# A DeltaNet and MLP-mixer kernel: 130 of the first 900 steps stand elsewhere in the order of issue

## The chip, the core and the metric

The kernel runs on one core of a Trainium2 chip. The metric is the device time of one execution in microseconds (us): 623.53 before, the median of three runs (623.19 to 623.9).

## What is computed

The reference is a DeltaNet recurrence on q, k, v (batch 4, heads 8, sequence 768, head width 48) with a gate beta, followed by an MLP mixer on its output, laid out as (4, 768, 384).

```python
for t in range(S):                      # k normalised to length 1
    y[:, :, t] = einsum('bhd,bhde->bhe', q[:, :, t], state)
    v_old = einsum('bhde,bhd->bhe', state, k[:, :, t])
    state += beta[t] * outer(k[:, :, t], v[:, :, t] - v_old)
x = y as (B, S, H*D)
u = x + (relu(x^T @ w_tok1) @ w_tok2)^T        # token part
out = u + relu(u @ w_ch1) @ w_ch2              # channel part
```

## The kernel before

**Tiling.** The recurrence is walked in chunks of 64 positions. A *unit* is two chunks (128 positions) of one batch for all heads, so there are 24 units, six per batch. For each unit the kernel makes products of keys and queries with themselves, inverts a triangular matrix per chunk and head, and then carries the state from one chunk to the next with small products (64x48 and the like). The mixer of a batch follows when its units are written; its channel part is a Strassen-like sum of fewer large products.

**What sets the order.** Every piece of work is a Python generator, a *job*, that issues a few instructions and then yields; each stretch between two yields is a *step*. A table of words at the end of the kernel function (`order = """..."""`, from L1779) says whose next step is issued: `i0*2` means two steps of job i0. The instructions of all steps go, in this order, into the queues of their engines, and every engine runs its queue in order: PE (products), DVE, ACT and POOL (elementwise work), SP (which issues the DMAs). A waiting instruction holds up all behind it on its engine. Steps are counted from 0 here: r8.5 is the sixth step of job r8.

**The jobs that matter here.**

- k*u*, v*u* load keys, queries and values by DMA (L420, L444); b loads beta (L252) and turns it with products and an ACT copy (L261).
- p*u* normalises the keys of a unit: squares on ACT (L539), sums on DVE (L542), roots on ACT (L547, L548), the factors cs on DVE (L551, L552), the scaled mask mb (L574, on DVE for the first units and on POOL later), the scaled keys (L592), and the turned keys and queries through PE (L562, L582) and ACT (L566, L587).
- c*x*, d*x*: the products of the two chunks of a unit (four steps of L511 on PE), and their masking out of PSUM on DVE (L517), in the fifth step.
- t*u* brings the masked products to the layout of the inversion (ACT L674, DVE L677, POOL L679; from t7 on by DMA through DRAM, L686), i*n* is the inversion, a chain on DVE of a product (L747) and a sum (L751) per step after a transpose (L731), f*u* brings the result back (ACT L697, DVE L703, POOL L706), h*u* and j*u* join the inverted blocks (PE L781, L794, L855, L896; ACT L785, L799, L822, L873).
- r*x* is the recurrence of a chunk: p_k (L924) on PE, rw_t on DVE (L931), products (L944, L948) on PE, a copy on ACT (L954), a second group of products (L962, L963) on PE, the state ss_t on DVE (L971), the output on ACT (L976). In a chunk with ten steps the first group is step 5 and the second step 7.
- w*n* loads a weight piece: DMA (L280), two ACT operations (L286, L287), a DVE shift (L289), a POOL addition (L293); pieces from w18 on have sums of pairs on DVE (L318) behind these.
- m0 is the mixer of batch 0, whose first four steps are the products L1597 (four each in the trace).
- x, z (L235, `keep_warm`) and Y (L245, `warm_tiles`) are products of zeros, whose result is never read.

The tables, buffers and functions are the same before and after; POOL also clears two tiles once, one for the turned blocks (L652) and z16 (L619), in the course of the first t and h steps. Tiles named "prep" in PSUM come from a pool of two buffers.

Of the kernel before, what the change touches and what calls it, by code (L numbers as in the profile page):

```python
# [23 lines left out]
def kernel(  # L24
# [41 lines left out]
    B, H, S, D = q.shape  # L66
# [117 lines left out]
    t11 = const.tile([128, NB, HB], FP32, name="t11")  # L184
# [17 lines left out]
    w1 = const.tile([128, NCH, DTOK], FP32, name="w1")  # L202
    w2 = const.tile([128, NDH, S], FP32, name="w2")
# [407 lines left out]
    t16 = spare[:, cuts[1] : cuts[2]].rearrange("s (q t b) -> s q t b", q=2, t=QB)  # L611
# [1175 lines left out]
    w6 p5 p3 p5 j0*3 f1*2 h1*5 j0*2 w8*2 w17 f2 h2*3 v0 t4*2 w17 r0*5 p6 h2*2 c5*2  # L1787
    v1 w11*2 j1 p5 k7*2 c5 k7 c5 r0 c5 r0*2 w14*2 v1 w11*2 k7*2 p7 d5*5 r1*5 w14*2
    p6*2 t5 j1 t5*2 r1*2 j1 j2 p7 h3*2 r1*3 p6*3 i1*2 r2*5 k8*2 f3*2 w9 k9*3 j1*2
    v2*2 i1*3 j2*2 r2*2 f3 i1*2 p6*3 w16 v2 w16*3 r2*2 h3 r2 i1 d6 r3*5 i1*2 w9*3  # L1790
    v2 d6 h3 v2 w0 h3*2 r3 h3 d6*2 w0 d6 j3 c6*5 r3*4 w0 j2 w0 p8*2 j2 r4 p8 r4*4
    k9*3 j3*2 r4*2 i1*2 w24 i1*2 p7*7 r4 c7 r4 r5*5 k10 p9 k10 p9 c7 r4 c7*3 i1
    w5*2 p7 r5*2 w24*3 r5*3 j3*2 i1 r6*4 w26 v3*5 p9 k11 r6 d7*5 w26*3 p8*3 t6*2
    r6*2 w5*2 p8*4 v4*2 t6 i1 r6*3 h5*2 h4*2 k10*2 f4*3 c8*2 k10 p10 w28*2 c8*2 r7
    c8 r7*3 d8*4 p9 d8 w28 h4*5 p9 t6 r7*2 j4 w28 p9*3 r7*2 p9 w7 d9 w7 v4*2 f5*2
    w27*2 w7*2 d9*4 c9*2 f5 c9*3 t7*2 t8 r7*2 t7*2 j4*2 v4 p10*2 h5 r8*3 w29 t8*3
    w29 w27*2 r8*2 w29*2 q3 w29 j4*2 r8 w22*4 t9*3 r8*3 p9 r9 p10 r9*3 t9 v5 h5*3
    j5 i2 r9 w4*2 r8 h5 i2*5 w4 i2 w19*2 k10 w32 p10*2 w32 v7 k12 m0*2 k11 k12 q0
    v5*3 p10*2 r9*2 j5*2 k11*3 i2*2 r9 w4 i2 j5 i2*3 p10 v5 r9*2 d10*3 r10 v7*2 j5
    i2*2 r10*4 w12 i2 k12 i2*2 m0 w32 k11 k12 w32 r10*2 m0 p11 k12*4 w19 p11 r10  # L1800
    c10 r10 c10 r10 w33 d10*2 q2 Y r11*4 v7 r11*3 w19 c10 q1 w30 c10 r11 k12*2
    i2*3 r11 v6*4 i2*5 m0*3 i2*5 q5 i2 m0 p11*4 c10 p11 m0 p11*2 m0*2 k12*2 w12
    m0*3 v6 f6*3 w12 d11 c11*2 d11*2 c11 w33 c11 d11*2 j6 p12 w12 m0 w33 w30*3
    p12*2 f7*3 j6*2 m0 c11 j7 f6 f8 w27*2 f8 j7 f8 w15 f7 m0 w29 w33 w29 j7 r12*4
    w31 j8 p11 t10*3 r12 Y r12 f9 j8 f9 w21 p12 r12 f8 r13*2 w15*2 r12 w15 r13*3
# [81 lines left out]
```

## Time and profile before

| | before |
|---|---|
| median of the runs | 623.53 us |
| the profiled execution | 626.48 us, span 624.7 |
| granted TensorE clock, mean | 0.973 |
| PE busy | 594.3 us (95%) |
| DVE busy | 466.1 us (75%) |
| ACT busy | 256.6 us (41%) |
| POOL busy | 110.2 us (18%) |

Times in the profile count from the span's start. A row of a timeline gives the start, the length, the engine, the line and the operation with what it writes and reads, and in brackets how long its engine had stood idle before it and what ended that. A row of the chain of waits gives the start and the length of a piece of the chain that ended last. A row of the stretches gives the stretch, the busy time of each engine, the granted clock (1.00 is full), the share of the DMA engines that was busy, and GB/s. In the first 125 us PE is not always busy, and its clock is cut in six windows of 3.4 us and multiples of it, from 29.6 us on.

### The profile page before, as it was taken

The page shows a single profiled execution, that of the slowest core. Times are in us where ns is not written, and L with a number is a line of the kernel's source. Part 1 is how long each engine was busy: PE and PEld are TensorE (multiplying, and loading weights), DVE is VectorE, ACT ScalarE, POOL GpSimd, SP SyncE. Part 2 cuts the span into 40 slices and gives each one's busy share as a digit, 9 for nine tenths or more (in the row PEclk, how much of TensorE's full clock was granted, in tenths as well). Part 3 has the DMA queues.
Part 4 walks back from the last instruction along what each step waited for, and adds up shares of the span by engine and source line. Part 5 has one row for each costly group of instructions (what it writes and reads, how often), then busy time and mean ns, then how long its engine had stood idle before and what let it go on. Part 6 is the DMA issues. An engine that isn't in the chain of part 4 may idle for free.

```text
span 624.7 us, 20909 instructions
## 1 busy us (share of the span) xinstructions
PE 594.3 (95%) x8733; PEld 519.7 (83%) x8733; DVE 466.1 (75%) x1160; ACT 256.6 (41%) x682; POOL 110.2 (18%) x150
## 2 busy tenths in 40 slices
PE   8489898899999999999999999999999999999998
PEld 5467776667898988977888888896699999999997
DVE  4986876986889845697567986866688898675874
ACT  7748787448522344213551305423252241404200
POOL 2346355215311121003020130011000000000000
PEclk9978897999999999999999999998999999999999
DMA  9566567657653244554544443134102012020001
GB/s 220 125 140 146 143 151 192 137 139 177 129 113 71 64 103 91 102 116 96 104 74 123 93 88 76 35 80 120 32 2 39 1 17 48 14 52 13 14 26 50
DMA packets 154605, 55.52 MB, mean 89 GB/s; under 512 B 129648, under 2 KB 148976, under 8 KB 154512
## 3 DMA queue, kind: packets, MB, share of 16 engines
q1 hardware_dynamic: 154512, 54.20, 38.3%
q8 instruction: 68, 1.11, 0.8%
q14 instruction: 25, 0.20, 0.1%
HBM read 41.19 MB, written 11.21 MB: 84 GB/s over the span
## 4 chain that ended last, share of the span: by engine, by line
PE 74%; DVE 10%; DMA 4%; ACT 3%; issue 2%; SPq 2%; POOL 0%; ACTq 0%; DVEq 0%
PE p_c L1672 13%; PE p_r L1502 13%; PE p_o L1693 10%; PE p_a L1574 6%; PE p_b L1574 6%; PE p_g L511 3%; PE p_h L1612 3%; DVE x L751 2%; PE p L1597 2%; DVE sub L747 2%; PE p_k L924 1%; DMA x<-n_dram 1%; PE p_h L1242 1%; PE p_s L962 1%; PE p_y L1038 1%
## 5 line engine op out<-in xcount | busy, mean ns | idle before, releaser
L1672 PE MATMUL p_c<-u_t,wc 128*128 128x256 f32 x432 | 101.6, 386 | 0.6 <-issue 0.6
L1672 PEld LDWEIGHTS p_c<-u_t,wc 128*128 128x128 f32 x432 | 79.6, 190 | 11.9 <-issue 1.1
L1693 PE MATMUL p_o<-wc,r 128*128 128x192 f32 x360 | 64.6, 331 | 0.7 <-DVE xb L1632 0.7
L751 DVE TENSOR_TENSOR x<-x,sub 128x84 f32<-128x84 f32 (+24 forms) x178 | 59.6, 335 | 6.1
L747 DVE TENSOR_TENSOR sub<-x 128x84 f32<-128x84 f32 (+24 forms) x178 | 57.7, 324 | 8.1 <-DMA x<-n_dram 3.5
L1693 PEld LDWEIGHTS p_o<-wc,r 128*128 128x128 f32 x360 | 58.4, 190 | 2.3 <-DVE xb L1632 1.3
L1681 ACT ACTIVATE r<-p_c 128x512 f32<-128x512 f32 x36 | 21.5, 596 | 49.3 <-PE p_c L1672 43.9
L511 PE MATMUL p_g<-kq 48*64 48x128 f32 (+1 forms) x704 | 35.2, 288 | 3.0 <-ACT kq L587 3.0
L517 DVE TENSOR_TENSOR gm<-p_g,mb 128x512 f32<-128x512 f32 x44 | 28.9, 684 | 9.5 <-PE p_g L511 8.4
L484 POOL TENSOR_TENSOR v_st<-v_st,nrm 128x384 f32<-128x384 f32 x12 | 11.2, 931 | 132.4 <-DMA v_st<-in_v_dram 104.8
L511 PEld LDWEIGHTS p_g<-kq 48*64 48x64 f32 (+1 forms) x704 | 27.1, 141 | 7.9 <-ACT kq L587 4.0
L574 POOL TENSOR_TENSOR mb<-mask_c,cs 128x512 f32<-128x512 f32 x20 | 21.2, 1061 | 65.3 <-DVE cs L552 35.7
L293 POOL TENSOR_TENSOR wc<-w_f,d 128x384 uint32<-128x384 uint32 x24 | 24.6, 1030 | 43.3 <-DVE w_f L289 20.2
L1502 PE MATMUL p_r<-t_d,wc 128*128 128x192 f32 x160 | 28.8, 326 | 0.0
L1515 DVE TENSOR_TENSOR kq<-kq,p_r 128x384 f32<-128x384 f32 x40 | 21.1, 552 | 10.2 <-PE p_r L1502 8.3
L1515 DVE TENSOR_TENSOR gm<-gm,p_r 128x384 f32<-128x384 f32 x40 | 21.2, 552 | 8.1 <-PE p_r L1502 5.8
L400 DVE STREAM_TRANSPOSE kq<-pads 128x512 f32<-128x512 f32 x24 | 25.6, 1109 | 1.6 <-DMA pads<-in_k_dram 1.2
L1502 PEld LDWEIGHTS p_r<-t_d,wc 128*128 128x128 f32 x160 | 26.5, 190 | 0.0
L1693 PE MATMUL p_o<-wc,s 128*128 128x192 f32 x144 | 25.7, 330 | 0.7 <-DVE xb L1632 0.7
L1502 PE MATMUL p_r<-pads,wc 128*128 128x192 f32 x128 | 25.4, 326 | 0.0
L1693 PEld LDWEIGHTS p_o<-wc,s 128*128 128x128 f32 x144 | 23.3, 190 | 1.3 <-DVE xb L1632 1.0
L1632 DVE TENSOR_TENSOR xb<-xb,p_o 128x192 f32<-128x192 f32 x42 | 14.7, 349 | 12.7 <-PE p_o L1693 12.3
(315 smaller groups left out, 1390.6 us busy)
## 6 DMA issues: line engine op xcount, KB each, us to landing
d<-in_moe_w_ch_dram SPq DMA_DIRECT2D x24, 384.0 KB, 3.9
v_st<-in_v_dram SPq DMA_DIRECT2D x96, 48.0 KB, 2.7
out_dram<-xb SPq DMA_DIRECT2D x23, 192.0 KB, 2.1
kst<-in_k_dram SPq DMA_DIRECT2D x64, 48.0 KB, 2.6
n_dram<-gm SPq DMA_DIRECT2D x72, 32.0 KB, 2.4
pads<-in_k_dram SPq DMA_DIRECT2D x24, 96.0 KB, 3.0
pads<-in_q_dram SPq DMA_DIRECT2D x24, 96.0 KB, 2.7
gm<-w_dram SPq DMA_DIRECT2D x72, 32.0 KB, 2.1
```

Source lines behind the costliest of these rows:

```text
L293: nc.gpsimd.tensor_tensor(out=dst.bitcast(U32), in0=f, in1=lo, op=ALU.add)
L400: nc.vector.transpose(kq_of[p // 2][:, i, :, p % 2].rearrange("f p (s g) -> f p g s", g=G), rows_of[i].rearrange("s p (g d) -> s p g d", g ...
L511: nc.tensor.matmul(p_g[PAR[i ^ cc ^ swap(u)], p], kqt[f, p, cc, 0], kqt[f, p, cc])
L517: nc.vector.tensor_tensor(out=blocks(gm_of(u))[:, :, cc, D:GW].rearrange("s p (two n) -> s p two n", two=2), in0=p_g, in1=made[u][:, :, cc ...
L747: nc.vector.tensor_tensor(out=tmp, in0=by[0].to_broadcast(list(to.shape)), in1=by[1].to_broadcast(list(to.shape)), op=ALU.mult,)
L751: nc.vector.tensor_tensor(out=to, in0=to, in1=tmp, op=ALU.add)
L1502: nc.tensor.matmul(p[:, i], pieces[q // width][:, at : at + 128], f[f"u{n}"], start=first and i == 0, stop=True, skip_group_check=True,)
L1515: nc.vector.tensor_tensor(out=o, in0=o, in1=p, op=op_of(sign))
L1574: nc.tensor.matmul(p, a[:, i], w[:, i // 2, i % 2], start=first and i == 0, stop=True, skip_group_check=True,)
L1672: nc.tensor.matmul(p_c[:, k], piece_of(wc1, cb, f * 128)[:, f * 128 : (f + 1) * 128], u_t[:, cb], start=(cb == 0), stop=(cb == NCB - 1),)
L1681: nc.scalar.activation(r2[:, m], p_c, ACTF.Relu)
L1693: nc.tensor.matmul(p, a[:, m], wc2[:, m, j], start=(start and i == 0), stop=(i == NM - 1), skip_group_check=True,)
```

## The change

The order table is written anew. It has the same 2610 steps, and each job's steps keep their order; 130 steps, all among the first 900, stand elsewhere, and behind step 869 the table is the same word for word. Of the table the diff shows three pieces.

```diff
     order = """
-    w10 x*4 z w10*2 z w1*4 k1*3 z k1*3 z b p1 z p1 k0*6 p0*2 b*2 p1 w2 p0*5 p1*2
+    w1*4 w10 x z w10*2 z k1*3 z x k1*3 z p1 z p1 k0 b k0*5 p0*2 b p1 b w2 p0*5
...
-    p4*2 t2*3 x t3*2 p4*2 x t3 i0*2 w13 p4*2 w18 w17*2 i0 k4 i0*9 p4 i0*2 p4*2 c4
-    k8 c4*3 w13*2 w6*2 k5*2 v0 k6 k5*2 i0*2 d4*2 k5 x z d4*3 c4 z*2 p5*2 k5 t4 p5
-    h0 h1 h0 w8*2 h1 Y i0 f0 Y p4 f1 h2*2 p5*3 f0*2 w6 h0*5 k6*5 p6 z f2*2 k8*3 p5
+    w18*2 i0*2 w13 p4*2 i0 k4 z*4 i0*8 w13 i0 w13 p4 w6 i0 w6 i0 p4*2 c4 k8 c4*3
+    k5*2 v0 k6 k5*2 i0*2 d4*2 k5 x d4 w8 d4 w8 d4 c4 p5*2 k5 t4 h0 h1 h0 p5 h1 i0
+    f0 p4 f1 p5 h2 p5 h2 p5 f2 f0*2 w6 f2 h0*5 k6*5 p6 k8*2 p5*2 k8 p5 w6 p3 j0*2
...
-    w29 w27*2 r8*2 w29*2 q3 w29 j4*2 r8 w22*4 t9*3 r8*3 p9 r9 p10 r9*3 t9 v5 h5*3
-    j5 i2 r9 w4*2 r8 h5 i2*5 w4 i2 w19*2 k10 w32 p10*2 w32 v7 k12 m0*2 k11 k12 q0
+    q3 w27*3 j4*2 r8 w29 t9*3 r8 t9 r8*2 w22 w29 m0*2 r8 w29 r8 p9 w29 r9*4 v5
+    h5*2 p10*2 h5 j5 r9 w22*3 i2 h5 i2 r8 i2 j5 i2 w4 i2 j5 i2 w4 i2 w4 k10 w19
...
```

At the first inversion POOL ran, before:

```order
L293 TENSOR_TENSOR wc_119<-w_f,d_282 128x384
L574 TENSOR_TENSOR mb<-mask_c,cs 128x512
L293 TENSOR_TENSOR wc_119<-w_f,d_403 128x384
L652 MEMSET r_124 128x32x16
L619 MEMSET z_571 128x2304
L592 TENSOR_TENSOR gm<-kst_98,cs 128x8x48
```

and now:

```order
L293 TENSOR_TENSOR wc_119<-w_f,d_276 128x384
L293 TENSOR_TENSOR wc_119<-w_f,d_403 128x384
L574 TENSOR_TENSOR mb<-mask_c,cs 128x512
L652 MEMSET r_124 128x32x16
L619 MEMSET z_583 128x2304
L592 TENSOR_TENSOR gm<-kst_98,cs 128x8x48
```

The first L293 is w18's, the one on d_403 w13's. w13's addition now stands ahead of p4's mask mb; and on DVE the shift that w13's addition waits for (L289 on d_403) moves from behind the inversion's step on 52 elements to behind its second step on 100 elements (L751 with shape 128x2x5x10).

On PE, around the joins of the first three units (h0 and h1 are the L781 on wc_120, h2 the one on gm), there stood before:

```order
L562 MATMUL p_t<-ident,pads 128x128 x4
L582 MATMUL p_t<-ident,pads 128x128 x4
L511 MATMUL p_g<-kq 64x128 x12
L235 MATMUL p_warm<-warm 128x128
L235 MATMUL p_warm<-warm 128x512
L511 MATMUL p_g<-kq 64x128 x4
L235 MATMUL p_warm<-warm 128x512 x2
L781 MATMUL p_z<-r_124,wc_120 64x32 x32
L245 MATMUL p_warm<-warm 64x128 x8
L781 MATMUL p_z<-r_124,gm 64x32 x16
```

and now:

```order
L245 MATMUL p_warm<-warm 64x128 x8
L235 MATMUL p_warm<-warm 128x128 x2
L562 MATMUL p_t<-ident,pads 128x128 x4
L235 MATMUL p_warm<-warm 128x512 x4
L582 MATMUL p_t<-ident,pads 128x128 x4
L511 MATMUL p_g<-kq 64x128 x12
L235 MATMUL p_warm<-warm 128x128
L511 MATMUL p_g<-kq 64x128 x4
L781 MATMUL p_z<-r_124,wc_120 64x32 x32
L781 MATMUL p_z<-r_124,gm 64x32 x16
```

The products of zeros that stood around and between the joins (z.6 to z.8 and Y, and behind them z.9) now stand ahead of or between p4's two transposes.

On PE, behind the first group of products of chunk r8, the difference has this piece:

```order
+L948 MATMUL p_w<-rw_t,gm 64x48
+L1597 MATMUL p_1877<-xb,w_117 128x384
+L1597 MATMUL p_1878<-xb,w_117 128x384
```

These are the first of m0's products, steps m0.0 and m0.1, which stood behind r9's p_k and p10's first transpose; steps m0.2 and m0.3, which stood between the products of r10, now stand ahead of r10.

More of the change, by code (lines that the diff above doesn't have):

```diff
@@ L1799 @@
[L1799 to L1805, printed above, removed]
@@ L1834 @@
-    f18 m1*3 c23*3 f20*2 f18 c23 f18*2 c23 f19*3 v18 r30 t22*4 c23 t23 r30*4 t23*3
+    w1*4 w10 x z w10*2 z k1*3 z x k1*3 z p1 z p1 k0 b k0*5 p0*2 b p1 b w2 p0*5
+    p1*2 w10 p0*2 x w3 w2 c0*3 p0 d0 c0 d0 p1 c0 d0*3 w2 k2*3 v1 p1*2 w18 k2*2 z
+    p1*2 c1*2 d1 k2 p2*2 c1 t0 d1 c1*2 d1*3 p2*3 t0 p2 w2 p2*2 Y p2*2 c2*2 d2
+    c2*3 d2 k3*6 p3 d2*2 p3 x d2 t1*3 p3*3 x p3*4 c3 k4*2 w3 k4 w3 k4*2 k7 w3 w13
+    d3*5 v1*2 v0*2 c3*3 v0 c3 Y*2 t0 p4*2 t2*3 x w18 t3*2 w17 p4 w17 p4 x t3
+    w18*2 i0*2 w13 p4*2 i0 k4 z*4 i0*8 w13 i0 w13 p4 w6 i0 w6 i0 p4*2 c4 k8 c4*3
@@ new lines @@
+    k9*3 j3*2 r4*2 p8*2 i1*2 w24 i1*2 p7*7 r4 c7 r4 r5*5 k10*2 p9*2 c7 r4 c7*3 i1
+    w5*2 p7 r5*2 w24*3 r5*3 j3*2 i1 r6*4 w26 v3*5 p9 k11 r6 d7*5 w26*3 p8*2 t6*2
+    r6*2 w5*2 p8*5 v4*2 t6 i1 r6*3 h5*2 h4 k10 h4 k10 f4*3 c8 k10 c8 p10 w28*2
+    c8*2 r7 c8 r7*3 d8*4 p9 d8 w28 h4*5 p9 t6 r7*2 j4 w28 p9*3 r7*2 p9 w7 d9 w7
+    v4*2 f5*3 w27 w7*2 d9*4 c9*5 t7*2 t8 r7*2 t7*2 j4*2 v4 p10 h5 r8*3 w29 t8*3
+    q3 w27*3 j4*2 r8 w29 t9*3 r8 t9 r8*2 w22 w29 m0*2 r8 w29 r8 p9 w29 r9*4 v5
+    h5*2 p10*2 h5 j5 r9 w22*3 i2 h5 i2 r8 i2 j5 i2 w4 i2 j5 i2 w4 i2 w4 k10 w19
@@ new lines @@
+    p10*2 j5 v7 k12 k11 k12 q0 v5*3 w32 p10 r9 p10 r9 k11 j5 k11*2 i2*2 r9 i2*3
+    m0*2 i2 w32 v5 w4 p10 w19 r9*2 r10 v7*2 i2*2 r10*3 d10*3 c10 r10*2 w12 i2 k12
+    i2*2 k11 k12 r10 p11 k12*4 r10*2 c10 w32 r10 w32 w33 d10*2 q2 Y r11*4 v7
+    r11*3 w19*2 c10 q1 w30 c10 r11 k12 p11 k12 i2*3 r11 v6*4 i2*5 m0*3 i2*5 q5 i2
+    m0 p11*4 c10 p11 m0 p11*2 m0*2 k12*2 w12 m0*3 v6 f6*3 w12 d11 c11*2 d11*2 c11
+    w33 c11 d11*2 j6 p12 w12 m0 w33 w30*3 p12 f7*3 j6*2 p12 m0 c11 j7 f6 f8 w27*2
+    f8 j7 f8 w15 f7 m0 w33 j7 r12*3 w29*2 j8 p11 t10*2 f9 r12 w31 f9 t10 r12 Y
@@ new lines @@
+    r12 j8 w21 p12 r12 f8 r13*2 w15*2 r12 w15 r13*3 w31*3 Y r13*2 w33 j8 w21 m0
+    r13 q4 p12*4 r13*2 m0*2 r14 c12 f9 j9 r14*2 w21 t10 w20*2 v7 r14*2 c12*2 w33
+    c12 r14 v8 c12*2 r14*2 w25*2 j9 r14 r15 v8 w21 r14 r15 w25 r15*3 w25 k13*4
+    w20 k13*4 p13 k13*2 w20 v8*3 m0*2 p13 w25 p13 m0 r15 p13 r15 p13 w27 w25
+    k13*2 j9 m0*4 p13 f9 w23 t12*3 p13 t12 w25 r15*3 c13*6 w23 k14*7 r16*5 m0 p13
+    m0*3 w23*4 k14 r16*2 t11 t13*2 j9*2 t11*3 w33 p14 r16*2 p14*2 w31 m0*3 w31 m0
+    w31 m0 w23 r17*2 r16 t13 r17 t13 r17*2 p14*2 m0*2 p14 i3 k14*4 i3*3 k15 v9*2
@@ new lines @@
+    m0*3 v10 i3*5 k15 i3 r17 k15*2 p14 k15*3 m0 v10*2 i3 k15*2 m0*2 k15*2 i3*4
+    r17*4 k15 i3*2 p14 m0*2 i3*6 m0*4 r18 i3 r18*2 v9*3 r18*2 i3*8 m0*10 v10*2 m0
+    r18 c14*4 r18*2 m0*2 f10 c14 f10*2 f12*2 p15*3 m0*4 r18 r19 r18 r19*3 j10 f10
+    j10*2 f12 p15 f11*4 f12 r19 c14 r19 v11 p15*3 k16*7 j11 m0*2 r19*4 j11 j12
+    r20*3 k16*2 r20 m0 r20 k16*3 v11 m0 j11 r20*2 v11*2 p15 c15*2 p10 r20*2 c15
+    r20 c15*3 f13*3 p16 r21*5 m0 r21*2 p16*4 k17*7 p16 j12*2 p16 k17 r21*3 m0*3
+    r22 c16 r22*3 k17*4 v11 r22 c16*4 r22*2 m0 r22 t14 p17 f13 c16 t14 j13*2 t14
```

86 lines of the change are left out of this document (33 added, 53 removed).

## The prediction

> **What bounds the kernel now.** I read the page first: the granted clock in 40 slices of 15.6 us, in tenths, and the chain of waits by engine.
>
> ```profile
> PEclk9978897999999999999999999998999999999999
> PE 74%; DVE 10%; DMA 4%; ACT 3%; issue 2%; SPq 2%; POOL 0%; ACTq 0%; DVEq 0%
> ```
>
> PE carries three quarters of the chain, and DVE a tenth. The clock is cut only in the first seven slices (to about 109 us) and once near 435 us. So I cut the start into stretches (columns: stretch, busy us of PE, PEld, DVE, ACT, POOL, granted clock, DMA share, GB/s).
>
> ```profile
> 30.00:40.00 10.00, 7.67 (x44) 4.37 (x44) 8.35 (x30) 3.70 (x7) 2.99 (x3) 0.68 0.80 166
> 40.00:50.00 10.00, 8.47 (x159) 7.49 (x160) 7.64 (x13) 6.70 (x19) 4.99 (x6) 0.83 0.57 127
> 100.00:110.00 10.00, 7.98 (x93) 5.73 (x90) 5.37 (x21) 5.49 (x17) 4.38 (x5) 0.56 0.72 210
> 130.00:140.00 10.00, 10.00 (x72) 6.79 (x70) 7.47 (x24) 4.60 (x11) 3.05 (x4) 1.00 0.41 108
> ```
>
> From about 125 us on PE is hardly ever idle and at full clock, and the order of all steps from there is unchanged (the last moved step, p12's, lies at 141 us). What the change does is therefore a shift of the moment when that full stretch begins. Before it the kernel runs from one latency to the next, and each move is worth what it does to the chain at its place. I add these up in order of time; minus is earlier.
>
> **1. The start, up to the first inversion (i0).** A pair of weight pieces changes place, some products of zeros stand later, w3's last steps move from 13 to 23 us, and w18's ACT step moves from ahead of p4 to just ahead of t3.
>
> ```profile
> 16.72 0.55 DVE L542 TENSOR_REDUCE ksum<-ksq 128x8 f32<-128x384 f32 x1 [0.46 <-ACT ksq L539]
> 23.20 0.58 ACT L286 ACTIVATE d<-d 128x384 f32<-128x384 f32 x1
> 23.65 0.58 ACT L287 ACTIVATE d<-d 128x384 uint32<-128x384 uint32 x1
> 25.82 0.63 ACT L674 COPY r<-gm 128x256 f32<-128x256 f32 x1 [0.65 <-DVE gm L517]
> 26.51 0.85 POOL L679 COPY r<-gm 32x256 f32<-32x256 f32 x1 [0.66 <-ACT nrm L547]
> ```
>
> DVE works without a gap from 17 us to i0; its 0.46 us gap at 16.26, which ACT causes, closes when w3's two ACT operations leave that stretch, and p1's normalisation ahead of beta's copy brings perhaps 0.24. That would be -0.7. But i0 waits for POOL's copy L679, which waits for ACT's L674; ACT's 0.65 us of idle ahead of it now has to hold w18's pair, 1.03 us from 23.20 to 24.23. I take **-0.45**, between -0.7 and 0.
>
> **2. Inside i0, up to the first products of h0.** Here POOL and DVE get in each other's way.
>
> ```profile
> 27.39 1.25 DVE L731 STREAM_TRANSPOSE x<-r 128x1024 f32<-128x1024 f32 x1
> 28.67 0.84 DVE L747 TENSOR_TENSOR sub<-x 128x28 f32<-128x28 f32 x1
> 29.54 0.21 DVE L751 TENSOR_TENSOR x<-x,sub 128x28 f32<-128x28 f32 x1
> 39.40 1.37 DVE L759 TENSOR_SCALAR r<-r,even 128x512 f32<-128x512 f32 x1 [0.79 <-ACT r L758]
> 40.69 1.27 DVE L517 TENSOR_TENSOR gm<-p_g,mb 128x512 f32<-128x512 f32 x2
> 27.44 1.01 POOL L293 TENSOR_TENSOR wc<-w_f,d 128x384 uint32<-128x384 uint32 x1
> 28.41 1.04 POOL L574 TENSOR_TENSOR mb<-mask_c,cs 128x512 f32<-128x512 f32 x1
> 37.01 1.06 POOL L293 TENSOR_TENSOR wc<-w_f,d 128x384 uint32<-128x384 uint32 x1 [7.56 <-issue]
> 38.48 2.01 POOL L619 MEMSET z<- 128x2304 f32 x1
> 40.46 0.99 POOL L592 TENSOR_TENSOR gm<-kst,cs 128x384 f32<-128x384 f32 x1
> ```
>
> L747 at 28.67 ends at 29.51, as POOL's mb does (29.45): 0.84 instead of 0.21, so +0.63. L759 ends 0.28 after the memset z, about 0.9 late. The transpose L731 beside L293 and the PSUM-fed L517 beside L592 are not held. Now w13's POOL addition goes ahead of mb and both stand after i0's tenth step, where two-operand additions run one behind the other: each holds one of them, as mb held L747, so +0.8 twice (1.0 less some 0.25). The 0.63 at 28.67 goes. POOL's chain then starts some three us earlier than its 37.01, and z is done before L759, whose 0.9 goes: -0.63 + 0.8 + 0.8 - 0.9 = **+0.1**. This assumes that the memset, which falls on L747 and L751 now, does not hold them. No row shows that pair. If it holds one as it held L759, it and the L592 behind it cost up to 2.7 more. I take no hold: what the memset held is one operand at double rate (512 elements in the 0.28 us after its end, where L517 takes 0.64), not a sum of two.
>
> The Trainium skill, "SBUF — State Buffer", section "Who interferes with whom", says that a two-input DVE instruction contends with a GpSimd instruction that reads SBUF and not with one that only writes, while `tensor_scalar` can enter a two-port mode that is blocked by any. The mb, z, L731 and L517 rows agree with it; by it the term is +0.1, by L759's row taken alone up to +2.8.
>
> **3. From h0 to the first recurrence.** The two tiles of zeros (L245) leave their place between h1 and h2 on PE.
>
> ```profile
> 41.51 2.21 PE p_z L781 x64
> 43.71 1.75 PE p_warm L245 x16
> 45.46 1.53 PE p_z L781 x31
> ```
>
> In the chain of waits they are 1.75. Yet the zeros z that filled PE until shortly before h0 are gone as well (moved ahead of p4's second transpose, into idle time), so h0 and h1 will meet a half clock: 31 products took 1.53 there, 64 would take 3.1 instead of 2.21, +0.9. And ACT, which copies h0, h1, h2 and f0 to f2, has its own row of work from there to the first recurrence; I let it keep half of the remaining 0.85: **-0.4**, between -1.75 and +0.5.
>
> **4. r3 and r4.** d6's masking on DVE (step d6.4) moves behind r3.8. The "prep" PSUM buffer that it empties is the one j2's product writes next.
>
> ```profile
> 73.00 0.69 DVE L517 TENSOR_TENSOR gm<-p_g,mb 128x512 f32<-128x512 f32 x1 [0.76 <-PE p_g L511]
> 74.54 0.34 DVE L971 TENSOR_TENSOR ss_t<-ss_t,p_s 128x192 f32<-128x192 f32 x1
> 74.32 0.43 PE L896 MATMUL p_x<-gm,zst 32*32 32x32 f32 x15
> 75.69 0.25 ACT gm L822
> 78.82 0.60 ACT kq L587
> 79.46 0.43 PE p_g L511 x4
> ```
>
> L971 ends at 74.88, L517 then at 75.57: L896 starts 1.25 later, and ACT's L822, which waits behind its own 75.69, some 0.8 later. ACT works without a gap from there to 79.42, and r5 queues behind that. i1's eighth step goes into DVE's idle time ahead of r3 in return, worth up to 0.45. I take **+0.8**, between +0.3 and +1.3.
>
> **5. The place of i2.** m0's first eight products stand now between r8's two groups of products (steps r8.5 and r8.7) instead of behind r9; j4's last copy no longer waits for w29's pair on ACT; t9's writes go ahead of w22's load on SP.
>
> ```profile
> 99.65 0.55 ACT L286 ACTIVATE d<-d 128x384 f32<-128x384 f32 x1
> 100.09 0.54 ACT L287 ACTIVATE d<-d 128x384 uint32<-128x384 uint32 x1
> 100.65 0.75 ACT L822 COPY gm<-p_x 32x256 f32<-32x256 f32 x2
> 106.87 5.06 PE L1597 MATMUL p<-xb,w 128*128 128x384 f32 x8
> 117.57 1.49 PE p L1597 x4
> 103.37 0.34 PE L962 MATMUL p_s<-rw_t,gm 64*64 64x48 f32 x1 [0.41 <-ACT rw_t L954]
> 107.09 0.20 DVE sub L747
> 97.87:101.28 3.41, 2.63 (x94) 2.31 (x88) 2.67 (x6) 3.25 (x10) 2.55 (x5) 1.00 0.70 163
> 101.28:104.69 3.41, 2.42 (x62) 1.87 (x58) 0.79 (x3) 2.10 (x7) 2.41 (x3) 0.50 0.27 46
> ```
>
> L822 comes 0.75 earlier, r8.5's products end near 101.0 at full clock, then the eight take 2 x 1.49 = 3.0: r8's second group starts near 104.0 instead of 103.37, +0.65. Full clock saves some 0.8 on it and on r9's first products. DVE then does w29's two sums, p10's two, j5's transpose and r9.4 (about 1.9, an estimate at 0.3 to 0.4 for each of five, as such rows here have it), and w22's shift, before i2's first step: about 107.4 instead of 107.09, **+0.3**. The data of i2, earlier now, no longer matter. Whether the clock is full decides this term: the stretch of 3.41 us with PE busy 2.63 was followed by one at 0.50. It becomes busier by the 0.75 and by the first of the eight, so I take full clock. At half, the eight take 5.06, r8.5 and r8's second group 1.6 more, and i2 starts 3.3 later.
>
> **6. m0's next eight products, and the end of i2.** They move from between r10's steps, where the second row above (1.49, at 117.57) is one of two on the chain, to idle time ahead of r10. That is 3.0 off PE's chain, but DVE's inversion i2 runs without a gap beside it and r12 waits for its result as well; DVE's sum of work there is the same. I take **-0.4**, between 0 and -1.2.
>
> Everything else (w14 behind r1, beta's load behind k's on SP, the reorderings by one place) I put at nothing: at each the engine waits for another anyway, DVE for ACT at the start, ACT for PE behind r1; without that cover they are about 0.3 each, which the range holds.
>
> Sum: -0.45 + 0.1 - 0.4 + 0.8 + 0.3 - 0.4 = -0.05. The profiled execution took 626.48 (span 624.7 and 1.78 around it), 2.95 above the median of 623.53; I apply the sum to the median: **623.5**, no change. What a measurement of this kernel can tell from none is about 0.2%, 1.25 us.
>
> **The rivals.**
>
> *The half clock goes (faster).* Zeros and real products now stand in idle time at 26 to 31 us and at 101 to 104 us. Against my terms, PE may also keep its clock in one more of the half-clock windows: each costs up to 1.7 of PE's work, a pair late in the full stretch 3.4.
>
> ```profile
> 432.42:435.83 3.41, 3.16 (x64) 2.63 (x65) 3.34 (x10) 0.48 (x1) 0.00 (x0) 0.50 0.15 34
> ```
>
> The windows near 432 follow from a shift of the work against the window's beat. With h0 and h1 at full clock as well (-0.9) the sum is -0.05 - 0.9 - 1.7 = -2.65: 620.9. Against it: PE is still idle before h0.
>
> *The eight products at half clock (slower).* They stand ahead of r8's second group, and if the clock is cut at 101 us as before, i2 starts 3.3 later than before instead of 0.3 later, everything behind it too: -0.05 + 3.0, 626.5. It decides as soon as the stretch before stays near its 2.63 busy of 3.41. For it: the products ahead are tiny and ACT's wait remains; against it, the 0.75.
>
> *The memset holds i0 after all.* Then h0 comes up to 2.7 later, of which ACT's row of work hides a good half: +1.2, 624.7.
>
> **How the numbers follow.** No change as summed 0.40 (my terms carry about 1.5 either way: 0.13 faster, 0.20 same, 0.07 slower); clock kept 0.26 (0.24 faster, 0.02 same); eight products at half clock 0.21 (0.03 same, 0.18 slower); memset 0.13 (0.01, 0.07, 0.05). Together faster 0.38, same 0.32, slower 0.30. The range takes in the clock's gain and most of its loss: 620.3 to 626.4; the forecast's own is 622 to 625.
>
> **What would show it.** Right: in the new profile h0's products start within 0.8 us of 41.5 with no row of L245 behind h1; L747 steps of 1.0 beside w13 and mb but none of 2.0 beside the memset; r4 about 0.8 later against r3 than before; m0's first eight in 3.0 with clock 1.00 around 101 to 108 us; i2's first step within 1 us of 107. Wrong: clock 0.5 over the eight products, or a shift at 125 us that the rest does not keep.

## The result, and the profile after

The changed kernel takes 630.5 us (median of four runs, 628.69 to 633.21), the kernel before 623.36 in the runs beside it: 1.0118 times as long, with a 95% interval of 1.0081 to 1.0155. The forecast was no change, 623.5 us with a range up to 626.4. The kernel is slower, and lies outside the range. Medians, here and below, are of all executions, while the ratios leave out those more than 1.5% above their kernel's fastest, so the two need not agree to the tenth of a per cent.

The profiled execution took 631.57 us (span 629.6), 5.1 more than that of before. Its granted clock by slices of 15.7 us, and its chain of waits by engine:

```profile
PEclk9966799779999999999999999999999999999999
PE 68%; DVE 9%; DMA 3%; issue 2%; SPq 1%; ACT 1%; DVEq 0%; ACTq 0%
```

Against the row of before, slices 3 to 5 (31 to 79 us) went from 7, 8, 8 to 6, 6, 7, and slices 8 and 9 (110 to 142 us) from 9, 9 to 7, 7; slice 7 (94 to 110 us) went from 7 to 9. Up to 112 us the kernel before was cut in five stretches, eight windows of 3.41 us in all and not six; the changed kernel is cut in five stretches up to 132 us, thirteen windows. The same stretches as in the prediction, in the changed kernel (stretch, busy us of PE, PEld, DVE, ACT, POOL, granted clock, DMA share, GB/s):

```profile
30.00:40.00 10.00, 4.32 (x38) 3.28 (x38) 8.53 (x26) 4.37 (x10) 5.24 (x5) 0.83 0.89 196
40.00:50.00 10.00, 8.87 (x136) 8.01 (x136) 7.20 (x12) 7.31 (x21) 4.35 (x5) 0.51 0.39 81
100.00:110.00 10.00, 8.22 (x192) 6.00 (x189) 4.57 (x16) 7.37 (x21) 4.12 (x5) 0.92 0.72 201
120.00:130.00 10.00, 8.50 (x182) 7.32 (x178) 9.23 (x23) 3.40 (x10) 2.01 (x2) 0.61 0.70 174
```

PE is busy for 4.32 us instead of 7.67 at 30 to 40 us, because the zeros left. Then the clock is 0.51 instead of 0.83 for the next ten. At 100 to 110 it is 0.92 instead of 0.56. The place where I feared the half clock got better, and two others got worse.

Step by step (the same step's start in both profiles, after minus before), the shift is:

| step | after minus before, us | gained or lost since the row above |
|---|---|---|
| i0's first | -0.58 | -0.58 |
| h0's first | -0.57 | 0.0 |
| r0's first products | +1.31 | **+1.9** |
| r5's first | +1.09 | -0.2 |
| i2's second | +1.38 | +0.3 |
| i2's sixth | +2.80 | **+1.4** |
| r14's first | +6.02 | **+3.2** |
| r35's first products | +7.7 | +1.7 |
| the end | +4.93 | -2.8 |

The last row is luck of this pair of profiles: the two half-clock windows that the profile of before has at 432 to 439 us do not occur in this one of after. Without them the shift is 7.7, near the 7.1 between the medians. The three bold rows are to be explained; the 1.7 behind r14 came bit by bit (+6.8 at r22) and I did not follow it further.

### The profile page after: what moved, and what is told of

It reads as the page before. It is cut to its first block, busy times and chain, and to the rows that moved or that the text cites. A ratio compares the mean times of both kernels' runs of the same rounds, so it can differ in the third digit from the quotient of the medians.

```text
span 629.6 us, 20913 instructions
## 1 busy us (share of the span) xinstructions
PE 598.0 (95%) x8733; PEld 523.5 (83%) x8733; DVE 469.5 (75%) x1160; ACT 257.0 (41%) x682; POOL 111.0 (18%) x150
## 4 chain that ended last, share of the span: by engine, by line
PE 68%; DVE 9%; DMA 3%; issue 2%; SPq 1%; ACT 1%; DVEq 0%; ACTq 0%
PE p_c L1672 13%; PE p_r L1502 12%; PE p_o L1693 10%; PE p_a L1574 6%; PE p_b L1574 6%; PE p_h L1612 3%; DVE sub L747 3%; DVE x L751 2%; PE p L1597 2%; PE p_g L511 2%; PE p_h L1242 1%; PE p_y L1038 1%; PE p_k L924 1%; PE p_s L962 1%; PE p L1227 1%
## 5 line engine op out<-in xcount | busy, mean ns | idle before, releaser
L747 DVE TENSOR_TENSOR sub<-x 128x84 f32<-128x84 f32 (+24 forms) x178 | 62.0, 348 | 7.4 <-DMA x<-n_dram 2.9
L751 DVE TENSOR_TENSOR x<-x,sub 128x84 f32<-128x84 f32 (+24 forms) x178 | 60.0, 337 | 6.1
L517 DVE TENSOR_TENSOR gm<-p_g,mb 128x512 f32<-128x512 f32 x44 | 29.0, 685 | 10.8 <-PE p_g L511 10.1
L293 POOL TENSOR_TENSOR wc<-w_f,d 128x384 uint32<-128x384 uint32 x24 | 24.7, 1031 | 48.7 <-ACT d L287 14.8
```

The lines of the kernel that those rows point to most:

```text
L293: nc.gpsimd.tensor_tensor(out=dst.bitcast(U32), in0=f, in1=lo, op=ALU.add)
L517: nc.vector.tensor_tensor(out=blocks(gm_of(u))[:, :, cc, D:GW].rearrange("s p (two n) -> s p two n", two=2), in0=p_g, in1=made[u][:, :, cc ...
L747: nc.vector.tensor_tensor(out=tmp, in0=by[0].to_broadcast(list(to.shape)), in1=by[1].to_broadcast(list(to.shape)), op=ALU.mult,)
L751: nc.vector.tensor_tensor(out=to, in0=to, in1=tmp, op=ALU.add)
```

## Three places in the trace

**From h0 to r0.** The changed kernel in stretches of 3.41 us, the clock's own beat:

```profile
36.79:40.21 3.42, 0.27 (x4) 0.00 (x0) 2.50 (x9) 1.26 (x3) 2.64 (x2) 1.00 0.89 219
40.21:43.62 3.41, 2.68 (x51) 2.71 (x52) 2.79 (x4) 2.06 (x6) 0.46 (x1) 0.50 0.66 117
43.62:47.03 3.41, 3.41 (x54) 3.23 (x52) 2.60 (x5) 2.76 (x8) 2.16 (x3) 0.50 0.01 1
47.03:50.45 3.42, 2.95 (x45) 2.27 (x45) 2.02 (x4) 2.74 (x7) 1.73 (x3) 0.50 0.48 125
50.45:53.86 3.41, 3.33 (x96) 3.04 (x93) 2.59 (x6) 2.27 (x8) 2.56 (x4) 0.50 0.63 107
53.86:57.27 3.41, 3.25 (x58) 3.25 (x60) 0.30 (x1) 1.73 (x7) 2.97 (x5) 0.50 0.68 159
```

PE is idle in the stretch ahead of h0 (0.27 of 3.42), and the next is cut, as the prediction had it. But it then stays cut for five windows, 17 us, though PE is busy for 2.68 to 3.41 us of each: at 43.62 it is busy throughout, and the next window is cut again. What runs there is mostly small, the joins' 64x32, 64x48 and 32x32 products; the only wide ones up to 55 us are two groups of transposes (L562, L582). Rows of the changed kernel's timeline, with the price:

```profile
40.94 3.63 PE L781 MATMUL p_z<-r,wc 64*64 64x32 f32 x64 [3.88 <-DVE gm L517]
46.20 1.11 PE L562 MATMUL p_t<-ident,pads 128*128 128x128 f32 x4
47.25 1.52 PE L794 MATMUL p_x<-wc,z 64*48 64x48 f32 x32
48.70 1.11 PE L582 MATMUL p_t<-ident,pads 128*128 128x128 f32 x4
55.78 1.04 PE L948 MATMUL p_w<-v_st,wc 64*64 64x48 f32 x16
```

Against the L794 stands this row of the chain of waits of the kernel before:

```profile
47.57 0.88 PE p_x L794 x32
```

h0 and h1 (L781) take 3.63 instead of 2.21, the 32 products of L794 take 1.52 instead of 0.88, and r0's L948 starts at 55.78 instead of 54.48 (the row of before is the first of the next fence).

**i2's first steps.** Before, in its timeline (the last row belongs to the third place):

```profile
54.48 1.06 PE L948 MATMUL p_w<-v_st,wc 64*64 64x48 f32 x16
107.54 0.22 DVE L747 TENSOR_TENSOR sub<-x 128x58 f32<-128x58 f32 x1
107.79 0.22 DVE L751 TENSOR_TENSOR x<-x,sub 128x58 f32<-128x58 f32 x1
125.39 2.85 PE L1597 MATMUL p<-xb,w 128*128 128x384 f32 x8
```

After:

```profile
102.79 2.85 PE L1597 MATMUL p<-xb,w 128*128 128x384 f32 x8
108.90 0.92 DVE L747 TENSOR_TENSOR sub<-x 128x58 f32<-128x58 f32 x1
109.85 0.96 DVE L751 TENSOR_TENSOR x<-x,sub 128x58 f32<-128x58 f32 x1
108.68 1.06 POOL L293 TENSOR_TENSOR wc<-w_f,d 128x384 uint32<-128x384 uint32 x1 [3.64 <-DVE sub L747]
109.70 1.04 POOL L574 TENSOR_TENSOR mb<-mask_c,cs 128x512 f32<-128x512 f32 x1
128.61 4.70 PE L1597 MATMUL p<-xb,w 128*128 128x384 f32 x8
134.89 0.55 DVE L1616 TENSOR_TENSOR xb<-xb,p_h 128x384 f32<-128x384 f32 x1 [1.43 <-PE p_h L1612]
```

w22's POOL addition and p10's mask run now, one behind the other, beside i2's second product and sum, and hold them as w13's and mb's hold i0's: 0.92 and 0.96 instead of 0.22 each, +1.4. m0's first eight products, at 102.79, take 2.85 at full clock.

**At 122 to 132 us.** m0's third eight (L1597 at 128.61) take 4.70 at half clock instead of 2.85, and DVE, which works i2 off in a row, stands 1.43 us waiting for m0's next product at 134.89. Ahead of that, i2's product on 234 elements (L747 at 126.46) takes 1.03 instead of 0.39 beside one more POOL addition (L293 at 126.23), another 0.64. The windows around it, and one that was followed by a cut earlier (105.03, with 0.50 from 108.45 on):

```profile
105.03:108.45 3.42, 2.24 (x72) 1.46 (x72) 2.03 (x8) 1.91 (x5) 0.01 (x1) 1.00 1.00 317
...
115.30:118.71 3.41, 2.18 (x7) 0.95 (x5) 3.20 (x7) 0.83 (x2) 1.65 (x2) 1.00 0.72 174
118.71:122.13 3.42, 1.75 (x64) 1.47 (x64) 3.25 (x10) 2.30 (x6) 0.00 (x0) 1.00 0.92 224
122.13:125.54 3.41, 2.92 (x74) 2.75 (x66) 2.95 (x9) 1.40 (x4) 0.87 (x1) 0.50 0.45 82
125.54:128.95 3.41, 3.15 (x56) 2.98 (x56) 3.27 (x8) 0.55 (x2) 1.15 (x2) 0.50 0.61 161
128.95:132.37 3.42, 3.42 (x6) 1.84 (x6) 3.15 (x9) 0.42 (x2) 0.00 (x0) 0.50 0.82 205
```

PE is busy for 1.75 of the 3.42 us ahead of the cut at 122.13: m0's second eight, which filled this place before, now run earlier.

## The experiments

The theory: what costs the time is the half clock from h0 to r0, and it comes from the products of zeros that the change took away there. The rivals: the second stretch of half clock, from m0's products that moved; POOL's operations beside i2; and d6's masking. The kernels below differ from the two above in the order alone, or by some more products of zeros. Times are medians, ratios are to the kernel before, run beside them (its medians were 622.27 us beside e1 to e4, 622.4 beside e5 to e8 and 622.68 beside e9 to e12).

**Zeros back in the change (e1).** The six steps of zeros that left this place (z.6 to z.9 and both of Y) stand where they stood before; everything else is as changed.

```diff
-    c3 Y*2 t0 ... i0 k4 z*4 i0*8 ... k5 x d4 w8 d4 w8 d4 c4 p5*2 k5 t4 h0 h1 h0 p5 h1 i0 f0 p4 f1 ... p6 k8*2
+    c3 t0 ... i0 k4 i0*8 ... k5 x z d4 w8 d4 w8 d4 c4 z*2 p5*2 k5 t4 h0 h1 h0 p5 h1 Y i0 f0 Y p4 f1 ... p6 z k8*2
```

> The changed kernel with only z.6 to z.9 and Y.1, Y.2 (the products of zeros around the first three joins) back at their places of before. In the changed kernel's profile PE was busy 0.26 of 3.41 us from 36.79 on, its clock then at half from 40.2 to 57.3 us, and the first recurrence 1.3 us later than before although h0 started 0.57 earlier. Clock theory: with the zeros back the half clock lasts one window there, the first recurrence starts 0 to 1 us earlier than before instead of 1.3 later, and the kernel gains 1.5 to 3 us on the changed one: 627.5 to 629. Rival, that the loss is one of waits in the order behind h0 (ACT's queue, POOL beside DVE): the zeros change nothing, 630.5; with their 1.75 us between h1 and h2 it may even lose.

Measured: 623.46, ratio 1.0020 (0.9990 to 1.0050). Its stretches and its r0:

```profile
40.00:50.00 10.00, 8.99 (x250) 7.78 (x250) 9.13 (x15) 9.17 (x26) 5.62 (x7) 1.00 0.43 91
50.00:60.00 10.00, 9.06 (x312) 8.33 (x308) 6.87 (x17) 9.22 (x28) 7.83 (x11) 1.00 0.76 172
```

```profile
51.55 0.62 PE L948 MATMUL p_w<-v_st,wc 64*64 64x48 f32 x16
124.75 2.85 PE L1597 MATMUL p<-xb,w 128*128 128x384 f32 x8
```

No window from 36 to 67 us is cut, r0 starts 4.2 us earlier than in the changed kernel, and r14 stands at +0.84 against before instead of +6.02. Putting the zeros back takes some 7 us off, more than the 1.5 to 3 expected: in this order nearly the whole loss hangs on them. The second stretch of half clock, at 122 to 132 us, is gone too (L1597 2.85), though nothing was changed there.

**The zeros alone, in the kernel before (e2).** The same six steps moved the other way.

```diff
-    c3 d3*3 ... i0 k4 i0*9 ... k5 x z d4*3 c4 z*2 p5*2 ... h1 Y i0 f0 Y p4 f1 ... p6 z f2*2
+    c3 Y*2 d3*3 ... i0 k4 z*4 i0*9 ... k5 x d4*3 c4 p5*2 ... h1 i0 f0 p4 f1 ... p6 f2*2
```

> The kernel before with only z.6 to z.9 and Y.1, Y.2 moved as in the change. Clock theory: PE idle ahead of h0, half clock for several windows from 40 us on, first recurrence 1 to 2.5 us later, time 624.5 to 626.5. Rival (order, not clock): the 1.75 us of zeros between h1 and h2 leave the chain, first recurrence earlier, time 622 to 623.4.

Measured: 623.19, ratio 1.0020 (0.9994 to 1.0046).

```profile
40.00:50.00 10.00, 7.91 (x133) 7.45 (x134) 7.68 (x11) 5.82 (x15) 5.51 (x6) 0.50 0.55 122
```

```profile
42.09 3.63 PE L781 MATMUL p_z<-r,wc 64*64 64x32 f32 x64 [7.59 <-DVE gm L517]
56.12 1.06 PE L948 MATMUL p_w<-v_st,wc 64*64 64x48 f32 x16
```

The clock goes in the same way (0.50, 3.63 for h0 and h1, r0 1.6 later than before), but by r14 only 1.08 of it is left, and the median is 0.9 us up, with an interval that includes no change. The clock and r0 came as the clock theory had them, the time as its rival had it. So the moved zeros make the half clock by themselves, but its price depends on the order around them: in the kernel before part of it is made good by r14 and nearly all in the median, in the changed one it grows by r14.

**m0's products back in the change (e3), and moved alone in the kernel before (e4).**

```diff
-    w22 w29 m0*2 r8 ... v7 k12 k11 ... i2*3 m0*2 i2 ... k12 i2*2 k11 k12 r10 p11
+    w22 w29 r8 ... v7 k12 m0*2 k11 ... i2*4 ... k12 i2*2 m0 k11 k12 r10 m0 p11
```

> The changed kernel with only m0's first four steps (16 products) back at their places of before. In the changed kernel's profile PE was busy 2.18 and 1.74 of 3.41 us from 115.3 and 118.7 on, where m0.2 and m0.3 used to stand, its clock then at half from 122.1 to 132.4, and m0.4 to m0.5, on the way of everything behind, took 4.70 instead of 2.85 us. Clock theory: no half clock from 122 to 132, 1.5 to 3 us less than the changed kernel: 627.5 to 629; the first eight products then stand in half clock again at about 107 to 112, which costs little. Rival (the i2 chain on DVE, held by POOL's additions, sets the end of this stretch): no change, 630.5, or up to 1 less.

Measured (e3): 630.85, ratio 1.0130 (1.0090 to 1.0169). This is the median of five executions; a sixth, of 1930.01 us, stands apart and is left out. No gain. The half clock from 40 us on is still there (0.52 at 40 to 50 us). Between 112 and 132 us only one window is cut now (118.9 to 122.3), and m0's third eight take 2.85, yet r14 stands at +5.14 instead of +6.02: mending the clock there does not mend the time.

```diff
-    t9*3 r8*3 ... v7 k12 m0*2 k11 ... j5 i2*3 ... i2*2 m0 w32 k11 k12 w32 r10*2 m0 p11
+    t9*3 r8 m0*2 r8*2 ... v7 k12 k11 ... j5 i2*2 m0*2 i2 ... i2*2 w32 k11 k12 w32 r10*2 p11
```

> The kernel before with only m0.0 and m0.1 moved behind r8.6 and m0.2, m0.3 moved ahead of r10, as in the change. Clock theory: PE empty between r9 and r10, half clock behind it, 1 to 3 us slower: 624.4 to 626.4. Rival (forecast's own step: the moved products fill idle time and leave r10's chain): 0 to 1 us faster, 622.4 to 623.4.

Measured (e4): 623.36, ratio 1.0018 (0.9981 to 1.0055). Its profile shows half clock at 118.8 to 125.6 us and r14 2.33 later than before, as the clock theory had it; the median is the rival's and does not tell it from nothing. m0's move alone is not the cause; that it makes a small loss is open.

**Other zeros in the idle stretch (e5).** The change as it is, with three more steps of zeros just ahead of h0, where PE stands idle for 3.88 us.

```diff
-    k5 t4 h0 h1 h0
+    k5 t4 z*3 h0 h1 h0
```

> The changed kernel with three steps of zeros (z, 128x512) added just ahead of h0 on PE, where it stands idle for 3.9 us in the changed kernel's profile; nothing else differs, and the three add work. Clock theory (the idle time ahead of h0 cuts the clock, and the small products behind it don't bring it back): the 17 us of half clock from 40 us on go or shrink to one window, the first recurrence comes 2 to 4 us earlier, and the kernel takes 623 to 626, as with the zeros back (623.46). Rival (it is the place of Y between the joins that matters, or DVE and ACT order): no change, 630 to 631, or later by the zeros' own 0 to 1.

Measured: 627.46, ratio 1.0080 (1.0046 to 1.0115).

```profile
40.00:50.00 10.00, 8.20 (x210) 7.37 (x212) 8.81 (x16) 9.02 (x25) 5.24 (x6) 0.83 0.42 92
120.00:130.00 10.00, 9.75 (x105) 7.11 (x98) 8.97 (x23) 2.31 (x7) 2.02 (x2) 0.56 0.56 145
```

Work was added and nothing taken away, and r0 starts 3.8 us earlier in the profile than in the changed kernel. No step moved and nothing waits for these products, so that is put down to the clock. The median is about 3 us lower (0.4% by the ratios, whose intervals overlap), between the two expectations. The stretch at 120 us stays at half clock (0.56), and the rest of the loss stays too.

**Half of the zeros back (e6: Y; e7: z).**

```diff
-    c3 Y*2 t0 ... h1 i0 f0 p4 f1
+    c3 t0 ... h1 Y i0 f0 Y p4 f1
```

> The changed kernel with only Y.1 and Y.2 back between h1 and h2; z.6 to z.9 stay moved. Clock theory, idle time ahead of h0 decides: half clock still from 40 us on, Y takes 1.75 us at half clock there, time 629 to 631.5. Rival, Y itself keeps the clock through the joins: 624 to 626.

```diff
-    k4 z*4 i0*8 ... k5 x d4 w8 d4 w8 d4 c4 p5*2
+    k4 z i0*8 ... k5 x z d4 w8 d4 w8 d4 c4 z*2 p5*2
```

> The changed kernel with only z.6, z.7 and z.8 back ahead of h0; z.9 and Y stay moved. Clock theory, idle time ahead of h0 decides: full clock at h0 and behind, 622.5 to 625 (without Y's 1.75 us even less than with all zeros back, 623.46). Rival, Y needed: 628 to 630.5.

Measured: Y back (e6) 626.39, ratio 1.0081 (1.0050 to 1.0112); z back (e7) 625.06, ratio 1.0047 (1.0017 to 1.0077). From e6:

```profile
42.30:45.80 3.50, 3.50 (x56) 3.50 (x54) 1.92 (x5) 2.84 (x8) 2.01 (x3) 0.50 0.12 24
45.80:49.20 3.40, 2.93 (x70) 2.42 (x67) 1.27 (x2) 2.47 (x8) 2.41 (x3) 1.00 0.36 114
```

and from e7:

```profile
40.00:50.00 10.00, 7.51 (x215) 6.89 (x216) 9.16 (x16) 8.68 (x24) 5.62 (x7) 0.92 0.42 93
50.00:60.00 10.00, 9.77 (x286) 9.44 (x281) 5.14 (x14) 8.08 (x26) 6.00 (x8) 0.74 0.73 169
```

Either half alone keeps part of the clock. z's steps ahead of h0 keep it from being cut there; without Y behind h1 it then goes at 48.3. With Y's two steps a clock that was cut comes back at 45.8; in the changed kernel, without them, it stays cut until 57.3. From Y alone I had expected at most 1.5 us, and it is worth about as much as the three new zeros of e5.

**The start alone, without the zeros (e8).** The first 300 steps as the change has them, the six steps of zeros at before's places, and everything behind step 300 as before. Against the changed kernel, the start differs so:

```diff
-    c3 Y*2 t0 ... i0 k4 z*4 i0*8 ... k5 x d4 w8 d4 w8 d4 c4 p5*2 ... h1 i0 f0 p4 f1 ... p6 k8*2
+    c3 t0 ... i0 k4 i0*8 ... k5 x z d4 w8 d4 w8 d4 c4 z*2 p5*2 ... h1 Y i0 f0 Y p4 f1 ... p6 z k8*2
```

> The kernel before with only the change's moves of the first 300 steps, without those of z.6 to z.9 and Y.1, Y.2. With the zeros back in the changed kernel the first recurrence came 2.9 us earlier than before, and the rest of the change gave 3.8 back by r14. If that rest (d6.4 behind r3.8, w22 and mb beside i2's first steps, m0's products) is what loses, this kernel keeps 1.5 to 3 us: 619.5 to 621. Rival: the gain of the start is absorbed by waits and half-clock windows further on whatever the order there, and the time is that of before, 622 to 623.

Measured: 620.48, ratio 0.9981 (0.9952 to 1.0010).

```profile
51.72 0.62 PE L948 MATMUL p_w<-v_st,wc 64*64 64x48 f32 x16
```

r0 starts 2.75 us earlier than before. By i2's nineteenth step this is gone in the profile, where m0's second eight meet a half clock (114.0 to 120.8). It has the lowest median of all kernels here, 1.9 us below before, but its interval includes 1, so it is not shown to be better.

**Zeros ahead of r10 as well (e9).** To e5, two steps of zeros in the idle time ahead of r10, for the second stretch.

```diff
-    w19 r9*2 r10 v7*2
+    w19 r9*2 z*2 r10 v7*2
```

> The changed kernel with three steps of zeros ahead of h0 (as in the run before) and two more ahead of r10, where PE stands idle for 2.4 us once m0.2 and m0.3 are gone from behind it. Clock theory: no half clock from 118 to 129 us, m0.4 and m0.5 again in 2.85 us, i2's end no later than its own DVE chain, 1.5 to 3 us less than with the three alone (627.46): 624.5 to 626. Rival (DVE's chain of i2, later by POOL's holds, sets that stretch): 627 to 628.5, since the two steps take 2.2 us of their own ahead of r10.

Measured: 626.82, ratio 1.0088 (1.0057 to 1.0119).

```profile
120.00:130.00 10.00, 9.38 (x95) 6.03 (x96) 9.45 (x25) 2.99 (x9) 2.02 (x2) 1.00 0.53 145
```

```profile
123.13 2.85 PE L1597 MATMUL p<-xb,w 128*128 128x384 f32 x8
```

In the profile the clock is whole at 120 to 130 us, and m0's third eight start 1.8 us earlier than in e5 and take 2.85 instead of 4.75. But r14 gains only 1.4 of it (+0.38 instead of +1.75), and the ratio is that of e5. The mechanism at the second place is seen; what it costs in the median is not settled.

**POOL's operations away from i2 (e10).** e1 with w22's steps and p10's mask back ahead of r9's end, so that POOL has done them before i2.

```diff
-    p10 h5 ... r8 w29 t9*3 r8 t9 r8*2 w22 w29 m0*2 r8 w29 r8 p9 w29 r9*4 v5 h5*2 p10*2 h5 j5 r9 w22*3 i2
+    p10*2 h5 ... r8 w29 w22 t9*3 r8 t9 r8*2 w29 m0*2 r8 w29 w22*3 r8 p9 w29 r9 p10 r9*3 v5 h5*3 j5 r9 i2
```

> The changed kernel with the zeros back (623.46) and, besides, w22's steps and p10's second and third step back ahead of r9, so that w22's POOL addition and p10's mb no longer stand beside i2's first steps. In the profiles L747 and L751 on 58 elements took 0.92 and 0.96 there instead of 0.23, and i2 fell 1.4 us behind between its first and fifth step. Theory, POOL holds DVE's two-input operations: i2's fifth step comes 1.2 to 1.5 us earlier, time 621.8 to 623. Rival (i2's start moves by as much, since w22's load is back ahead of t9's writes): the time stays at 623 to 624.

Measured: 625.7, ratio 1.0047 (1.0010 to 1.0084): not faster than e1 (623.46), if anything slower. From i2's second step to its sixth 0.45 us are lost against before, instead of e1's 0.88, but another hold of 0.4 remains (L747 on 30 elements takes 0.64), and the clock is cut at 118.4 to 128.7, where in e1 it was not. So POOL's hold is in the trace, and removing about half of it brought nothing; the time lies above both expectations, and why is open.

**More zeros in the better start (e11).** e8 with four steps of zeros between p4's transposes, one ahead of r8's second group and one ahead of r10.

```diff
-    i0 k4 i0*8 ... t9*3 r8*3 ... d10*3 r10
+    i0 k4 z*4 i0*8 ... t9*3 r8 z r8*2 ... d10*3 z r10
```

> The kernel before with the change's moves of the first 300 steps and the zeros where they were (620.48), plus six more steps of zeros in PE's idle time: four between p4's transposes, one ahead of r8's second group, one ahead of r10. Clock theory: fewer half-clock windows at 29 to 39, 100 to 107 and 114 to 121 us, 0.5 to 2.5 us less: 618 to 620. Rival (those windows stand where DVE is the bound, and the zeros delay r8 and r10): 620.5 to 622.

Measured: 623.55, ratio 1.0028 (0.9995 to 1.0061). In its profiled execution the clock is 0.989 and r12 comes 4.5 us earlier than before; it took 620.54, but that was the lowest of twelve runs that spread to 628.51. Against e8's 620.48 the zeros added here brought nothing, and the time lies above both expectations: zeros do not help everywhere.

**d6's masking alone (e12).** The kernel before with d6's fifth step behind r3's ninth.

```diff
-    h3 d6*2 w0 d6 j3 c6*5 r3*4 w0 j2 w0 p8*2
+    h3 d6*2 w0 j3 c6*5 r3*4 w0 j2 w0 d6 p8*2
```

> The kernel before with only d6's masking step moved behind r3.8, as in the change. Forecast's own step: j2's product waits for the PSUM buffer, r4 comes 0.8 to 1 us later and r5 1 us later, and that stays: 623 to 624 beside 622.4 of before. Rival: PE idles there anyway, nothing is left at r5: 622.4.

Measured: 621.97, ratio 1.0012 (0.9977 to 1.0047).

```profile
73.32 0.69 DVE L517 TENSOR_TENSOR gm<-p_g,mb 128x512 f32<-128x512 f32 x1 [1.23 <-PE p_g L511]
74.09 0.35 DVE L971 TENSOR_TENSOR ss_t<-ss_t,p_s 128x192 f32<-128x192 f32 x1
74.56 0.69 DVE L517 TENSOR_TENSOR gm<-p_g,mb 128x512 f32<-128x512 f32 x1
74.07 0.69 PE L896 MATMUL p_x<-gm,zst 32*32 32x32 f32 x32
```

j2's product L896 starts at 74.07, half a microsecond before the later L517 begins. It waits for the first L517, and not for the moved one. The fourth term of the prediction has no mechanism.

## Why the prediction was wrong

By its own six terms, with what the profiles show from the table of shifts:

| term | forecast | measured | |
|---|---|---|---|
| 1 the start up to i0 | -0.45 | -0.58 | right |
| 2 inside i0 | +0.1 | 0.0 | right, by its parts |
| 3 from h0 to the first recurrence | -0.4 | +1.9 | failed |
| 4 r3 and r4 | +0.8 | -0.2 | mechanism absent |
| 5 the place of i2 | +0.3 | +0.3, and +1.4 not seen | half |
| 6 end of i2 | -0.4 | +3.2 | failed |

**Term 2** held in each of its parts. The changed kernel's timeline around i0's end:

```profile
34.26 1.06 DVE L751 TENSOR_TENSOR x<-x,sub 128x88 f32<-128x88 f32 x1
35.35 0.95 DVE L747 TENSOR_TENSOR sub<-x 128x72 f32<-128x72 f32 x1
36.61 0.21 DVE L747 TENSOR_TENSOR sub<-x 128x52 f32<-128x52 f32 x1
39.71 0.49 DVE L759 TENSOR_SCALAR r<-r,even 128x512 f32<-128x512 f32 x1 [0.79 <-ACT r L758]
36.62 2.01 POOL L619 MEMSET z<- 128x2304 f32 x1
```

w13's addition and mb (POOL, 34.20 to 36.21) hold two steps to 1.06 and 0.95. The memset beside 36.61 holds none (0.21), and L759, free of it, takes 0.49 instead of 1.37. The pair that no row of before showed thus came out as the Trainium skill has it, "SBUF — State Buffer", section "Who interferes with whom": a POOL operation that only writes does not hold a sum of two.

**Term 3** is the step that failed. It said that "h0 and h1 will meet a half clock" and priced it at 0.9, as if it ended with them. h0 and h1 lost 1.4, and everything up to r0 ran on at half clock, five windows long. Y, which I counted as 1.75 us on the chain to be saved, was what brought the clock back (e6) or kept it (e7 loses it behind h1). The bound of +0.5 left room for little more than h0 and h1, so the range ended too low. The rule of the Trainium skill, "TensorE: Matmul & The Clock Gate", "Part 1: The HAM clock gate", by which one busy window of 3.4 us releases the clock, does not describe these rows: at 43.62 PE was busy for 3.41 of 3.41, and the next windows were granted 0.50.

**Term 4** rested on which L517 j2's product waits for, read from the shared buffer's name and not from the trace. e12 shows the product starting ahead of the moved one.

**Term 5** was right where I thought it most in doubt: the clock is 0.92 at 100 to 110 us, the eight products take 2.85, r8's second group comes 0.8 later than its chunk's shift alone would have it (I said 0.65), and i2 begins with the shift that it inherits. It missed that i2 then runs beside w22's addition and p10's mask. The prediction lists w22's shift on DVE and does not ask where its POOL addition falls, though the row of mb at 28.41 had given the price of such a meeting in its second term. e10 does not show a gain from undoing it, so in the median it may be worth nothing.

**Term 6** took the place ahead of r10 as idle time to be filled for nothing, and did not ask what the place that was emptied does to the clock. With m0's second eight gone PE is busy 1.75 of 3.42 us, the clock is cut, and the third eight take 4.70. Of the +3.2, the wait at 134.89 is 1.43 and the POOL addition beside i2 another 0.64. Not asking is the same mistake as in term 3. But the runs qualify what the clock does here: m0 back alone gains nothing, with one cut window left (e3), m0 moved alone loses nothing that can be measured (e4), and in e1 the stretch is whole with m0 moved. Its loss appears where the work arrives at another phase or later, and how much of the median belongs to it stays open (e9: full clock there, same median as e5).

Of the rivals, "the eight products at half clock" had the right mechanism at the wrong place. Of the signs listed, h0 at 40.94 (within 0.8 of 41.5), the L747 rows and the eight at full clock came as for right; r4 came no later against r3, and i2's first step at 108.47 is 1.38 late; the shift of 3.6 at 126 us that grew to 6.0 by r14 was the sign for wrong. The premise that from 125 us on PE is at full clock was part of the order that was changed.

With the rest of the change in place, nearly all of the loss is shown to come from the zeros, by e1 (7 us). That they act through the clock is seen in the profiles of e5, e6 and e7; of their ratios only e7's lies clear of the changed kernel's. The mean granted clock of every execution says the same: on average it is 0.978 before (94 executions), 0.965 in the changed kernel (4), 0.978 in e1, and 0.973, 0.971 and 0.974 in e5, e6 and e7. But an equal clock is not an equal time: e9 has the 0.978 of before and takes 626.82, and e2 takes 623.19 with 0.972. So the order has a part in the price that the clock alone does not give. What stays open: that part; how the 7 us divide between the start and the stretch at 122 to 132 us; why the zeros alone cost no more than 0.9 in the kernel before (e2); and why e11's early gain does not reach its median.

## What to carry to other kernels

Products of zeros in idle time can be load-bearing: in these profiles they hold the clock ahead of a chain of small products, and bring it back between small products. Before moving any filler, zeros or real work, out of a gap on PE, look at the window of 3.4 us that is emptied, and price a cut clock as lasting until a window that PE fills, and longer where small products fill it, not as one window. A POOL operation that reads is to be kept away from the steps of a DVE chain (0.7 us each here), and which instruction waits for which is to be read from starts in the trace, not from the name of a pool.

## What the runs showed that was not expected

- A window in which PE is fully busy with small products need not restore the clock (3.41 of 3.41 at 43.62 to 47.03 us, then 0.50 three times more). It is the exception: counted in the traces of all fourteen kernels up to 600 us, 62 windows at half clock had PE busy for 3.40 us or more, 56 of them were followed by full clock and six were not; no window with under 2.99 was. In the six, products of 128 columns or more took 1.45 us at most, in the 56 at least 1.30. So the width fits but gives no sharp bound, and no run tested it by itself.
- Busy time tells the cut only at its ends: in the same count of windows at full clock, all 25 with PE busy for less than 1.7 us were followed by a cut one and none of the 1998 with 3.0 or more. Between these both occur: stretches with 1.75 and 2.24 of 3.42 were followed by a cut one, so was one with 2.63 before, and at 115.30 to 118.71 us in the changed kernel 2.18 was not.
- One and the same kernel spreads by 2%: 98 runs of the kernel before lie between 615.96 and 628.29 us, where the first three lay within 0.7. Executions differ in where the windows fall (the pair at 432 to 439 us is there or not), and a profiled execution lay up to 3 us from its kernel's median (626.48 against 623.36 for before, 620.54 against 623.55 for e11). The prediction's 0.2% is too fine for this kernel: even ten to twelve runs leave an interval of 0.3 to 0.4% either way.
